# One order for all five queues, weight words joined in pairs, one reciprocal per head pair, and a warm-up

## The chip, the cores and the metric

The kernel runs on one core of one Trainium2 chip. The metric is the device time of one execution in microseconds (us); lower is better. The engines are named as in the profile: PE (TensorE matmul), PEld (its weight loads), DVE (VectorE), ACT (ScalarE), POOL (GpSimd) and SP (SyncE, which issues nearly all DMA transfers here).

## The reference, cut to what matters

Three stages follow each other: windowed attention, a dense gated block, and a top-1 mixture of eight experts.

```python
scores = q @ k.T / 8, masked to 0 <= i-j < 64       # 4 batches, 8 heads, 576 tokens, 64 dims
x = softmax(scores) @ v                             # as [2304, 512]
x = ((x @ w1) * (x @ w2)) @ w3 @ w_out              # weights arrive as 64-bit floats
e = argmax(x @ w_gate); gate = softmax(x @ w_gate)[e] * sigmoid(x @ w_output_gate)[e]
out = gate * (relu(x @ ew1[e]) @ ew2[e])
```

## The kernel before, in words

**The dense block.** `w3 @ w_out` is multiplied once into one matrix, `w34`. Tokens go in six units (u = 0 to 5) of 384. For each unit and each of eight column blocks m, `gate` (L565) makes `x @ w1` and then `x @ w2` in two PSUM banks (tag `ab`), ACT keeps the first (`a_sb`, L570), DVE multiplies (L573), ACT and DVE write the product as a high and a low part (L577, L581), and `down` (L589) multiplies it by `w34`. Every float32 product is three passes over high and low parts.

**The weights.** `w_out`, `w3`, `w1` and `w2` come in 40 transfers of 512 KB (`fetch`, L494), of 64-bit words. For each, DVE joins float32 values out of the two halves of a word in three operations over 512 elements (`convert`, L511, L513, L518), through a PSUM bank of tag `ab`; ACT writes the high part (L532) and POOL the low part (L536). The product `w34` is made of the 24 transfers of `w_out` and `w3` (L545). `w1` takes over the SBUF of the raw `w3` words and `w2` that of the finished `w_out`, so `w2` is written only when the product is complete; then the units start.

**Attention.** There are 16 head pairs, four for each batch. One pair has three groups g: scores (L149 adds the mask in the matmul, L153), a row maximum on DVE (L162, L165), exponentials on ACT (L175), sum plus 1e-9 and its reciprocal on DVE (L185, L187, once per group), the product on POOL (L192), a transpose on PE and its copy on ACT (L199, L204), and with v the output (L216) in PSUM, of which ACT and DVE write high and low parts into the units' `x` tiles (L228, L232). `x` has three buffers, so unit u shares one with unit u+3. Pairs 4 to 7 (batch 1) write into units 1 and 2. Two buffers each hold q, k and v: the load of v for pair n waits until the output of pair n-2 is done.

**Routing.** Every token's row is scattered into the DRAM buffer `xs`, from which the experts read. Before that, 32 transfers of 257 KB (`clear`, L813) fill the head of every expert's part with blank rows.

**Order.** A planner (`Plan`) keeps a list of steps with an engine, a length, a rank, and buffers that it takes and gives back, and emits them in the order in which it would start them. Before, PE alone kept that order (`manual_schedule(engines={E.PE})`); the instructions of DVE, ACT, POOL and SP were placed anew by the framework's own scheduler. An engine runs its instructions strictly in the order in which they stand, and SP's transfers are issued in order too: one that waits holds those behind it.

Of the kernel before, what the change touches and what calls it, by code (L numbers as in the profile page):

```python
# [29 lines left out]
NTILE = NT // 128  # L30
NEG = -1.0e30
RING = 3
NB = S // 64
VW = NB * 128

# [83 lines left out]
class Attention:  # L119
# [11 lines left out]
    def __init__(self, tc, pool, ps_s, ps_v, qkv, xunit, ident):  # L131
        self.tc, self.nc, self.pool, self.ps_s, self.ps_v = tc, tc.nc, pool, ps_s, ps_v
        self.qkv, self.xunit, self.ident = qkv, xunit, ident
        self.s = {}
        self.idb, self.mask = masks(tc.nc, pool, ident)
# [31 lines left out]
    def exps(self, n, g):  # L167
        nc, s = self.nc, self.s[n]
        ps = s["S", g]
        nm = s.pop(("nm", g))  # L170
        p = s["p", g] = self.pool.tile([128, self.GW], F32, name="pp", tag="pp", bufs=3)
        rs = s["rs", g] = self.pool.tile([128, 3], F32, name="rs", tag="rs", bufs=4) if n < self.SUMS else None
        for i in range(3):
            o = slice(128 * i, 128 * i + 128)
            nc.scalar.activation(out=p[:, o], in_=ps[:, o], func=AF.Exp, bias=nm[:, i:i + 1], scale=0.125,  # L175
                                 **({} if rs is None else dict(accum_out=rs[:, i:i + 1])))

    def recip(self, n, g):
        nc, s = self.nc, self.s[n]
        ps = s.pop(("S", g))  # L180
        rs = s.pop(("rs", g))
        if rs is None:
            rs = ps[:, 392:395]
            nc.vector.tensor_reduce(out=rs, in_=s["p", g].rearrange("p (a b) -> p a b", a=3), axis=AX, op=ALU.add)
        nc.vector.tensor_scalar(ps[:, 400:403], rs, 1e-9, None, op0=ALU.add)  # L185
        r = s["r", g] = self.pool.tile([128, 3], F32, name="r", tag="r", bufs=4)
        nc.vector.reciprocal(out=r, in_=ps[:, 400:403])  # L187
# [46 lines left out]
    def plan(self, P, n, r, done):  # L234
# [8 lines left out]
        for i, x in enumerate("qkv"):  # L243
            add(x, "DMA", (1.5, 0.8, 1.5)[i], -18 + i, self.load, (), i, take=[(x, (x, n))], lat=2.0)
        for g in range(3):
            q = -12 + 2 * g
            late = n >= self.LATE
            add(("sc", g), "PE", 0.38 if late else 0.55, q, self.score, N("q", "k"), g, take=[("S", ("S", n, g))],
                give=[("q", n), ("k", n)] if g == 2 else [])
            add(("top", g), "DVE", 1.28 if late else 0.72, q, self.top, N(("sc", g)), g)  # L250
            add(("exp", g), "ACT", 1.65 if n < self.SUMS else 1.02, q, self.exps, N(("top", g)), g, take=[("pp", ("pp", n, g))])
            add(("rec", g), "DVE", 0.4 if n < self.SUMS else 0.9, q, self.recip, N(("exp", g)), g, give=[("S", n, g)])
            add(("nor", g), "POOL", 0.85, q, self.normal, N(("rec", g)), g)
# [17 lines left out]
def masks(nc, pool, ident):  # L271

    idb = pool.tile([128, 128], BF16, name="idb")
    nc.vector.tensor_copy(idb, ident)
    mask = [pool.tile([128, 3, 128], BF16, name=f"mask{x}") for x in range(2)]
    nc.gpsimd.memset(mask[1], 0.0)
    for h in range(2):

        a = mask[1][64 * h:64 * h + 64]
        nc.gpsimd.affine_select(out=a, in_=a, pattern=[[0, 3], [1, 128]], compare_op=ALU.is_ge,  # L280
                                fill=NEG, base=-1, channel_multiplier=-1)
        nc.gpsimd.affine_select(out=a, in_=a, pattern=[[0, 3], [-1, 128]], compare_op=ALU.is_ge,
                                fill=NEG, base=64, channel_multiplier=1)
    nc.gpsimd.tensor_copy(mask[0], mask[1])
    nc.gpsimd.memset(mask[0][:, 0, 0:64], NEG)
    return idb, mask
# [127 lines left out]
def attention_moe_moe_kernel(ctx: ExitStack, tc: tile.TileContext, q0, k0, v, w1, w2, w3, w_out,  # L414
# [13 lines left out]
    ps_ab = pool(ctx, "ps_ab", bufs=2, space=PSUM)  # L428
    ps_acc = pool(ctx, "ps_acc", bufs=UT, space=PSUM)
    ps_s = pool(ctx, "ps_s", bufs=2, space=PSUM)  # L430
    ps_v = pool(ctx, "ps_v", space=PSUM)

# [14 lines left out]
    make_identity(nc, ident)  # L447
    gates = const.tile([128, 4, 16], F32, name="gates")
    rt = Router(tc, const, xs)

    moe = pool(s_moe, "moe")
    pa = pool(s_pa, "pa")
    att = pool(s_att, "att", side="right")
# [10 lines left out]
    at = Attention(tc, att, ps_s, ps_v, (q0, k0, v), xunit, ident)  # L464
    for src, c in ((w_gate, 0), (w_ogate, 8)):
        nc.sync.dma_start(out=gates[:, :, c:c + 8], in_=src.rearrange("(k p) e -> p k e", p=128))
    P = Plan(dict(q=2, k=2, v=2, S=2, pv=1, ab=2, acc=UT, pp=3, PT0=1, PT1=1, PT2=1, ck=RING, f=3, ck2=3,
                  w3T=3, a_sb=2, gt=2, x2=3, x2T=1))
# [6 lines left out]
    STAGED = {"wo": 8, "w3": 8}  # L475

    seq = [("wo", 0), ("w3", 0), ("wo", 1), ("wo", 2), ("wo", 3), ("w3", 2), ("wo", 4), ("w3", 1), ("wo", 5),
           ("wo", 6), ("wo", 7)]
    seq += [("w3", j) for j in range(3, 16)] + [("w1", j) for j in range(4)]
    seq += [(x, j) for j in range(8) for x in ("w2", "w1") if x == "w2" or j > 3]  # L480
# [4 lines left out]
    def fetch(i):  # L485
        kind, c = seq[i]
        if c < STAGED.get(kind, 0):
            t = stage[kind][c // 4][:, 1024 * (c % 4):1024 * (c % 4) + (1024 if wide else 512)]
            t = t.bitcast(I32 if wide else F32)
        else:  # L490
            t = ckp.tile([128, 1024 if wide else 512], I32 if wide else F32, name="ck", tag="ck", bufs=RING)
        raw[i] = t
        src = half[kind][c]
        nc.sync.dma_start(out=t, in_=src.bitcast(I32) if wide else src)  # L494
# [7 lines left out]
    def convert(i, step):  # L502

        if not wide:
            if step == 2:
                f32s[i] = raw.pop(i)
            return
        word = raw[i].rearrange("p (c t) -> p c t", t=2)
        if step == 0:
            bits[i] = ps_ab.tile([128, 512], F32, name="bits", tag="ab").bitcast(I32)  # L510
            V.tensor_scalar(bits[i], word[:, :, 1], 3, 0x3FFFFFFF, op0=ALU.logical_shift_left, op1=ALU.bitwise_and)  # L511
        elif step == 1:
            V.scalar_tensor_tensor(out=bits[i], in0=word[:, :, 1], scalar=-0x40000000, in1=bits[i],  # L513
                                   op0=ALU.bitwise_and, op1=ALU.bitwise_or)
        else:
            del raw[i]
            f32s[i] = ckp.tile([128, 512], F32, name="f", tag="f", bufs=3)
            V.scalar_tensor_tensor(out=f32s[i].bitcast(I32), in0=word[:, :, 0], scalar=29, in1=bits.pop(i),  # L518
                                   op0=ALU.logical_shift_right, op1=ALU.bitwise_or)
# [3 lines left out]
    def parts(i):  # L523
        kind, c = seq[i]
# [6 lines left out]
    def high(i):  # L531
        nc.scalar.activation(out=parts(i)[0], in_=f32s[i], func=AF.Copy)  # L532

    def low(i):
        hi, lo = parts(i)
        nc.gpsimd.tensor_tensor(lo, f32s.pop(i), hi.bitcast(F32), op=ALU.subtract)  # L536
# [22 lines left out]
    def gate(u, m, k):  # L559
        x, w = xunit(u), ws[("w1", "w2")[k]]  # L560
        ps = gps[u, m, k] = ps_ab.tile([128, 512], F32, name="ab", tag="ab")[:, 0:UNIT]
# [202 lines left out]
    def plan_chunk(i, kind, c):  # L764
        r = 5 + 2.4 * i
        staged = c < STAGED.get(kind, 0)
        key = ("ck", i)
        L = P.add("DMA", 1.4, r - 10, lambda: fetch(i), take=() if staged else [("ck", key)], lat=2.0)
        old = [done["mm", x, 3] for x in range(16)] if kind == "w2" else []
        t0 = P.add("DVE", 0.6, r, lambda: convert(i, 0), [L] + old, take=[("ab", ("b", i))])  # L770
        t1 = P.add("DVE", 0.6, r, lambda: convert(i, 1), [t0], lat=0)
        t2 = done["read", kind, c] = P.add("DVE", 0.6, r, lambda: convert(i, 2), [t1], take=[("f", ("f", i))],
                                           give=[("b", i)] + ([] if staged else [key]))
        after = [t2] + ([done["read", "w3", x] for x in range(8)] if kind == "w1" else [])
        hi = P.add("ACT", 0.63, r + 2, lambda: high(i), after, take=[("w3T", ("w3T", c))] if kind == "w3" else [])
        done[kind, c] = P.add("POOL", 1.28, r + 3, lambda: low(i), [hi], give=[("f", i)])

    def plan_w34(c, r):
        m, g = divmod(c, 2)
        for j in range(4):  # L780
            done["mm", c, j] = P.add(
                "PE", 0.71, r, lambda j=j: w34_mm(c, j), [done["w3", c], done["wo", 4 * g + j]]
                + ([done["mm", c - 1, 3]] if g else []),
                take=[("acc", ("accw", m))] if g == 0 and j == 0 else [], give=[("w3T", c)] if j == 3 else [])
# [5 lines left out]
    for n in range(NP):  # L790
        at.plan(P, n, 24 + 11 * n, done)
    for i, x in enumerate(seq):
        if x[0] != "w2":
            plan_chunk(i, *x)
    for c in range(16):
        plan_w34(c, 11 + 2.4 * seq.index(("w3", c)))
# [4 lines left out]
    def start_mo():  # L801
# [3 lines left out]
        z = blank[0] = mo[0].tile([128, RW], F32, name="x2", tag="x2", bufs=3)  # L805
        nc.gpsimd.memset(z[:, 0:DM], 0.0)
        nc.gpsimd.memset(z[:, DM:RW], float(NT))

    blank = [None]

    def clear(e, j):
        r = NS * e + 128 * j
        nc.sync.dma_start(out=xs[r:r + 128, :], in_=blank[0])  # L813

    def side(u):
# [3 lines left out]

    mo_open = P.add("SP", 0.0, 0, start_mo, [done["mm", x, 3] for x in range(16)], lat=0)  # L820
    done["clear"] = [P.add("DMA", 1.45, 106 + 3 * i, lambda i=i: clear(*divmod(i, 4)), [mo_open],
                           take=[] if i else [("x2", "blank")], give=["blank"] if i == 4 * NE - 1 else [])
                     for i in range(4 * NE)]
# [55 lines left out]
    def plan_end():  # L879

        o = P.add("SP", 0.0, 0, open_exp, [done["x", n] for n in range(B * NP)], lat=0)
        for j in range(11):
            done["el", j] = P.add("DMA", 1.4, 400 + 5 * j, lambda j=j: eload(j + 1), [o], take=[("ck2", ("ck2", j))], lat=2.0)
        for j in range(8):

            k, c = divmod(j, 4)
            old = [done["gate", NU - 1, 2 * c + 1, k - 1]] if k else []
            h = P.add("ACT", 1.06, 400 + 5 + 5 * j, ehigh, [done["el", j]] + old + ([done["es", j - 1]] if j else []))
            done["es", j] = P.add("DVE", 1.22, 400 + 5 + 5 * j, elow, [h], give=[("ck2", j)])
# [253 lines left out]
```

## Time and profile before

| | |
|---|---|
| median of 3 runs | 767.65 us (766.26 to 767.84) |
| the profiled execution | 768.43 us, its span 766.6 us |
| mean granted TensorE clock | 0.987 of full |
| busy: PE, DVE, ACT, POOL | 721.9 (94%), 370.9, 296.8, 165.0 us |
| unit 0's first gate starts, its last down is followed at | 98.79 us, 171.45 us |
| moved by DMA | 105.76 MB |

Busy time counts an engine's instructions; a PE that is busy may still run at half its clock, and matmuls overlap each other. What is lost on PE shows as idle time before an instruction with the name of what ended it, and as a matmul that takes longer than its fellows. A transfer has an issue on SP's queue and a landing, which is later by the time that the transfers in front of it take.

### The profile page before, as it was taken

To read this page: it belongs to the slowest core of one execution; us is meant where nothing else is said; L and a number is where in the kernel's file an instruction comes from. 1 tells how busy PE (TensorE), PEld (TensorE's weight loads), DVE (VectorE), ACT (ScalarE), POOL (GpSimd) and SP (SyncE) were. 2 spreads that over 40 slices of the span, in tenths; PEclk is the share of its full clock that TensorE was granted. 3 is DMA by queue.
4 is the path that set the end of the run, shared out by engine and by line. 5 is a ranking of instruction groups with operands and counts; after the bars stand their busy time and mean duration, and the time that the engine had idled before them with its cause. 6 is when DMAs were issued, how large, how long until landed. Compare 5 with 4: busy or idle time off the path is not lost. (4 is left out here: it accounts for less than half of the span.)

```text
span 766.6 us, 12408 instructions
## 1 busy us (share of the span) xinstructions
PE 721.9 (94%) x4630; PEld 644.8 (84%) x4630; DVE 370.9 (48%) x862; ACT 296.8 (39%) x697; POOL 165.0 (22%) x230
## 2 busy tenths in 40 slices
PE   3689899999999999999999999999999999999996
PEld 2568688989999989999999998878888897988875
DVE  6797668533255645574532233645255461671101
ACT  2466354541134334333411213446354463563121
POOL 5455444300111211131010010432112011111010
PEclk9899899999999999999999999999999999999999
DMA  8858588960112322210500011476546772740000
GB/s 333 344 193 285 200 241 276 272 187 3 42 48 81 107 94 81 80 73 1 192 30 14 1 70 40 160 246 225 187 144 209 239 247 76 255 157 28 4 29 27
DMA packets 39393, 105.76 MB, mean 138 GB/s; under 512 B 5388, under 2 KB 5388, under 8 KB 39312
## 3 DMA queue, kind: packets, MB, share of 16 engines
q1 hardware_dynamic: 36112, 95.27, 37.9%
q0 software_dynamic: 3200, 9.46, 3.1%
q8 instruction: 45, 0.74, 0.4%
q14 instruction: 36, 0.29, 0.1%
HBM read 86.83 MB, written 18.93 MB: 138 GB/s over the span
## 5 line engine op out<-in xcount | busy, mean ns | idle before, releaser
L565 PE MATMUL ab<-xt,w 128*128 128x384 f32 x1152 | 219.5, 341 | 2.7 <-DVE f L518 2.3
L565 PEld LDWEIGHTS ab<-xt,w 128*128 128x128 f32 x1152 | 199.4, 189 | 5.2 <-DVE f L518 2.5
L589 PE MATMUL acc<-w,gt 128*128 128x512 f32 x432 | 112.2, 403 | 0.7 <-ACT gt L577 0.7
L589 PEld LDWEIGHTS acc<-w,gt 128*128 128x128 f32 x432 | 79.5, 190 | 17.5 <-DVE gt L581 1.0
L933 PE MATMUL yps<-w,hT 128*128 128x512 f32 x336 | 82.6, 396 | 0.0
L192 POOL TENSOR_TENSOR pp<-pp,r 128x384 f32<-128x384 f32 x48 | 40.0, 834 | 157.3 <-DVE r L187 64.2
L933 PEld LDWEIGHTS yps<-w,hT 128*128 128x128 f32 x336 | 61.3, 188 | 11.8
L573 DVE TENSOR_TENSOR a_sb<-ab,a_sb 128x384 f32<-128x384 f32 x48 | 26.7, 557 | 90.8 <-PE ab L565 84.5
L175 ACT ACTIVATE pp<-sps,nm 128x128 f32<-128x128 f32 x144 | 46.8, 368 | 50.4 <-DVE nm L165 50.4
L545 PE MATMUL wps<-w,w3T 128*128 128x512 f32 x192 | 53.2, 423 | 12.3 <-ACT w3T L532 12.1
L690 DVE TENSOR_TENSOR w<-ck,w 128x1024 fp32r<-128x1024 f32 x45 | 54.4, 1221 | 20.4 <-ACT w L686 19.7
L686 ACT ACTIVATE w<-ck 128x1024 fp32r<-128x1024 f32 x48 | 50.1, 1057 | 18.5 <-DMA ck<-in_moe_w 16.6
L577 ACT ACTIVATE gt<-a_sb 128x384 fp32r<-128x384 f32 x48 | 25.1, 523 | 82.9 <-DVE a_sb L573 82.8
L925 POOL DMA_INDIRECT out<-y,idx x20 | 19.6, 979 | 173.8 <-ACT y L924 119.7
L545 PEld LDWEIGHTS wps<-w,w3T 128*128 128x128 f32 x192 | 36.8, 201 | 20.4 <-ACT w3T L532 12.1
L957 PEld LDWEIGHTS hps<-exT,w 128*128 128x128 f32 x384 | 46.3, 192 | 4.9 <-issue 3.1
L957 PE MATMUL hps<-exT,w 128*128 128x256 f32 x384 | 47.3, 284 | 3.2 <-PEq L1086 1.4
L570 ACT ACTIVATE a_sb<-ab 128x384 f32<-128x384 f32 x48 | 23.6, 492 | 57.2 <-PE ab L565 56.3
L204 ACT ACTIVATE PT<-tps 128x384 f32<-128x384 f32 x48 | 23.5, 493 | 46.4 <-PE tps L199 46.4
L438 DVE TENSOR_TENSOR exT<-gps,exT 128x512 fp32r<-128x512 f32 x23 | 15.8, 691 | 52.4 <-ACT exT L437 52.4
L153 PE MATMUL sps<-k,q 128*128 128x128 f32 x288 | 41.1, 282 | 0.0
L153 PEld LDWEIGHTS sps<-k,q 128*128 128x128 f32 x288 | 39.1, 198 | 0.6
(137 smaller groups left out, 1014.2 us busy)
## 6 DMA issues: line engine op xcount, KB each, us to landing
ck<-in_moe_w SPq DMA_DIRECT2D x88, 512.0 KB, 4.5
q<-in_q SPq DMA_DIRECT2D x16, 576.0 KB, 5.6
v<-in_v SPq DMA_DIRECT2D x16, 576.0 KB, 3.9
xs<-x SPq DMA_DIRECT2D x32, 257.0 KB, 8.7
xg<-xs SPq DMA_DIRECT2D x29, 257.0 KB, 3.0
k<-in_k SPq DMA_DIRECT2D x16, 320.0 KB, 6.2
w<-in_moe_w_out SPq DMA_DIRECT2D x8, 512.0 KB, 8.5
w<-in_moe_w SPq DMA_DIRECT2D x8, 512.0 KB, 9.8
```

The lines of the kernel that those rows point to most:

```text
L153: nc.tensor.matmul(ps[:, 128 * i:128 * i + 128], lhsT=s["q"][:, 128 * c:128 * c + 128], rhs=s["k"][:, 64 * c:64 * c + 128], start=late, st ...
L175: nc.scalar.activation(out=p[:, o], in_=ps[:, o], func=AF.Exp, bias=nm[:, i:i + 1], scale=0.125, **({} if rs is None else dict(accum_out=r ...
L192: nc.gpsimd.tensor_tensor(p, p, s.pop(("r", g)).unsqueeze(2).to_broadcast([128, 3, 128]), op=ALU.mult)
L545: mm(ps, lhsT=t[:, a, 128 * j:128 * j + 128], rhs=wo[b][:, o:o + 512], start=g == 0 and j == 0 and x == 0, stop=g == 1 and j == 3 and x == 2)
L565: mm(ps, lhsT=w[a][:, c:c + 128], rhs=x[:, b, kk, :], start=kk == 0 and i == 0, stop=kk == 3 and i == 2)
L573: V.tensor_tensor(asb[u, m], gps.pop((u, m, 1)), asb[u, m], op=ALU.mult)
L577: nc.scalar.activation(out=g[:, 0, :], in_=asb[u, m], func=AF.Copy)
L589: mm(accs[u][t], lhsT=g[:, a, 128 * t:128 * t + 128], rhs=ws["w34"][b][:, 512 * m:512 * m + 512], start=m == 0 and i == 0, stop=m == 7 and ...
L686: nc.scalar.activation(out=eparts()[0], in_=eq[0], func=AF.Copy)
L690: low.tensor_tensor(lo, eq.popleft(), hi.bitcast(F32), op=ALU.subtract)
L933: mm(ps, lhsT=hT[f][:, a, c0:c0 + 128], rhs=w[b][:, 512 * f:512 * f + 512], start=f == 0 and i == 0, stop=f == 7 and i == 2)
L957: mm(ps[:, 0:256], lhsT=w1e[a][:, c:c + 128], rhs=xT[:, b, kk, 0:256], start=kk == 0 and i == 0, stop=kk == 3 and i == 2)
```

## The change

- All queues follow the planner up to the last unit (`manual_schedule` for DVE, ACT, POOL and SP as well). Its ranks are new: the first pairs from rank 12 at steps of 6.1, pairs 4 to 7 from 68, unit 0 from 61, unit 1 from 134, and what follows 40 earlier.
- `w3` and `w_out` words are joined two transfers at a time: the first two operations run over 1024 elements in two PSUM banks of their own (`bits`), given up for `ab` when all of `w3` and `w_out` is read; the third stays at 512.
- Pairs 0 to 7 have one sum plus 1e-9 and one reciprocal over nine columns in place of three over three.
- The blank rows come from the `x` tile of unit 2, filled at the start, not from a tile that exists once the product is complete. `done["free", 2]` makes the first writes into that `x` tile wait for all 32 clears.
- Twelve matmuls on zeros run at the start; the small gate weights are loaded on ACT's queue; the masks are built without DVE; four buffers for the exponentials in place of three; the second half of expert 0's weights waits for the last column block of unit 5.

```diff
+WARM = 12
...
+CLEAR = 94
+MERGE = True
+CH = 2.47
+A0, DA0, A1, DA1 = 12, 6.1, 68, 9.6
+U0, DU0, U1 = 61, 10, 134
...
+        if one:
+            add("rec", "DVE", 0.36, -8, self.recip, N(*[("exp", g) for g in range(3)]), 2, give=[("S", n, 2)])
...
+        for _ in range(WARM):
+            mm(cold, lhsT=warm[:, 0:128], rhs=warm, start=True, stop=True)
...
+        t = P.add("DVE", us, r, lambda: convert(i, 0), L, take=[(tag, ("b", i))], lat=0)
+        t = P.add("DVE", us, r, lambda: convert(i, 1), [t], lat=0)
+        for c in cs:
...
+            t = done["read", kind, c] = P.add("DVE", 0.69, r, lambda c=c: join(i, c), [t],
+                                              take=[("f", ("f", i, c))], give=give, lat=0)
...
-        z = blank[0] = mo[0].tile([128, RW], F32, name="x2", tag="x2", bufs=3)
...
+    blank = xunit(2).rearrange("p a b c -> p (a b c)")[:, 0:RW].bitcast(F32)
...
+    done["clear"] = [P.add("DMA", 0.75, CLEAR + i, lambda i=i: clear(*divmod(i, 4))) for i in range(4 * NE)]
+    done["free", 2] = P.add("SP", 0.0, 0, lambda: None, done["clear"], lat=0)
...
-    done["clear"] = [P.add("DMA", 1.45, 106 + 3 * i, lambda i=i: clear(*divmod(i, 4)), [mo_open],
...
-    plan_unit(0, 100, 8)
-    plan_unit(1, 166, 6.5)
+    plan_unit(0, U0, DU0)
+    plan_unit(1, U1, 6.5)
...
-    P.run()
+    with tc.manual_schedule(engines={E.DVE, E.Activation, E.Pool, E.SP}):
+        P.run()
```

On SP's queue, from pair 5's q load on (`xs` is a clear, `ck` and `w0` weight transfers, `q`, `k`, `v` loads of attention), the changed kernel has:

```order
L881 DMA xs_57<-xt2_152 128x514
L152 DMA q_726<-in_q0 128x1152
L152 DMA k_742<-in_k0 128x640
L881 DMA xs_57<-xt2_152 128x514 x11
L152 DMA v_856<-in_v 128x1152
L881 DMA xs_57<-xt2_152 128x514 x7
L539 DMA ck_932<-in_moe_w1 128x1024
L881 DMA xs_57<-xt2_152 128x514 x2
L539 DMA ck_969<-in_moe_w2 128x1024
```

Nineteen of the clears stand ahead of `w1`'s fourth transfer here, and the last of the 32 stands behind `w2`'s fourth. Before, the first clear stands behind `w2`'s fourth transfer:

```order
L494 DMA ck_979<-in_moe_w2 128x1024
L494 DMA ck_1010<-in_moe_w2 128x1024
L494 DMA ck_1021<-in_moe_w2 128x1024
L494 DMA ck_1134<-in_moe_w2 128x1024
L813 DMA xs_57<-x2_1067 128x514 x6
L141 DMA q_1264<-in_q0 128x1152
L494 DMA ck_1173<-in_moe_w2 128x1024
```

So the clears moved ahead of the `w2` transfers that they followed. On ACT, about the first gates of unit 0 (`a_sb` is the kept first product, `w2` the high part of `w2`, `xt2` and `xt1` the `x` of units 2 and 1, `gt` the high part of the product), the changed kernel has:

```order
L624 ACTIVATE a_sb_1186<-ab_1133 128x384
L586 ACTIVATE w2_1149<-f_1160 128x512
L245 ACTIVATE xt2_152<-pvt_1163 128x64
L245 ACTIVATE xt1_378<-pv_1162 128x192
L245 ACTIVATE xt2_152<-pv_1162 128x320
L586 ACTIVATE w2_1149<-f_1205 128x512
L631 ACTIVATE gt_1236<-a_sb_1120 128x384
```

Pair 4's pieces of `x`, whose first goes into the tile of the blank rows, stand ahead of the first `gt` of unit 0, and that first piece waits for the landing of the last clears on all the DMA semaphores. Before, two `gt` stand ahead of them, and they wait for PE alone:

```order
L577 ACTIVATE gt_1216<-a_sb_1106 128x384
L532 ACTIVATE w2_1124<-f_1184 128x512
L204 ACTIVATE PT_1235<-tps3_1223 128x384
L532 ACTIVATE w2_1124<-f_1221 128x512
L577 ACTIVATE gt_1255<-a_sb_1150 128x384
L175 ACTIVATE pp_1259,rs_1260<-sps_1229,nm_1253 128x128 x3
L228 ACTIVATE xt1_359<-pv_1268 128x192
L228 ACTIVATE xt2_1312<-pvt_1269 128x64
L228 ACTIVATE xt2_1312<-pv_1268 128x320
```

The pieces moved up past unit 0's first `gt`, and gained a wait.

## Rows read from the trace of the kernel before

**Rows 1.** Waits of PE up to 172 us: total us, times, longest
```profile
PE wps L545 <- ACT w3T L532: 12.1, 1, 12.1
PE tps L199 <- POOL pp L192: 8.4, 4, 3.7
PE ab L565 <- DVE f L518: 2.3, 1, 2.3
```

**Rows 2.** Timeline of PE: start us, us, instructions, idle before
```profile
12.09 2.15 PE L545 MATMUL wps<-w,w3T 128*128 128x512 f32 x3 [12.09 <-ACT w3T L532]
...
92.51 0.90 PE L199 MATMUL tps<-ident,pp 128*128 128x128 f32 x3 [3.69 <-POOL pp L192]
93.06 5.13 PE L545 MATMUL wps<-w,w3T 128*128 128x512 f32 x12
...
98.79 2.36 PE L565 MATMUL ab<-xt,w 128*128 128x384 f32 x12
...
104.10 0.83 PE L153 MATMUL sps<-k,q 128*128 128x128 f32 x6
...
111.00 2.35 PE L589 MATMUL acc<-w,gt 128*128 128x512 f32 x9
113.28 1.15 PE L216 MATMUL pv<-PT,v 128*64 128x64 f32 x32
...
171.45 2.25 PE L565 MATMUL ab<-xt,w 128*128 128x384 f32 x12
```

**Rows 3.** Stretches: length, busy us (instructions) by engine, clock, DMA share, GB/s
```profile
15.00:30.00 15.00, 8.44 (x43) 6.07 (x41) 13.27 (x30) 8.00 (x28) 9.94 (x9) 0.87 1.03 421
...
90.00:105.00 15.00, 12.49 (x62) 10.94 (x63) 6.09 (x17) 4.68 (x18) 4.98 (x7) 0.77 0.59 180
```

**Rows 4.** Timeline of DVE: the first weight transfer, and a reciprocal
```profile
5.93 0.69 DVE L511 TENSOR_SCALAR bits<-w 128x512 int32<-128x512 int32 x1 [4.97 <-DMA w<-in_moe_w_out]
...
20.25 0.17 DVE L187 RECIPROCAL r<-sps 128x3 f32<-128x3 f32 x1
```

**Rows 5.** Groups of instructions: busy us, mean ns of one, idle before
```profile
L690 DVE TENSOR_TENSOR w<-ck,w 128x1024 fp32r<-128x1024 f32 x45 | 54.4, 1221 | 20.4 <-ACT w L686 19.7 <-PE hps L957 0.7
L573 DVE TENSOR_TENSOR a_sb<-ab,a_sb 128x384 f32<-128x384 f32 x48 | 26.7, 557 | 90.8 <-PE ab L565 84.5 <-PE tps L199 3.5 <-PE rps L375 2.7
L581 DVE TENSOR_TENSOR gt<-a_sb,gt 128x384 fp32r<-128x384 f32 x48 | 29.5, 615 | 11.8 <-ACT gt L577 11.7
L162 DVE TENSOR_REDUCE sps<-sps 128x3 f32<-128x384 f32 x48 | 26.7, 560 | 7.1 <-PE sps L153 6.8
```

**Rows 6.** DMA issues of the whole run: count, KB each, median us to landing
```profile
ck<-in_moe_w SPq DMA_DIRECT2D x88, 512.0 KB, 4.5
q<-in_q SPq DMA_DIRECT2D x16, 576.0 KB, 5.6
v<-in_v SPq DMA_DIRECT2D x16, 576.0 KB, 3.9
xs<-x SPq DMA_DIRECT2D x32, 257.0 KB, 8.7
...
k<-in_k SPq DMA_DIRECT2D x16, 320.0 KB, 6.2
```

**Rows 7.** A stretch in which seven clears, one v and one q are issued, columns as above
```profile
140.00:150.00 10.00, 10.00 (x91) 9.18 (x90) 3.68 (x12) 3.68 (x13) 2.44 (x3) 1.00 1.06 250
```

**Rows 8.** Timeline of SP's queue: start us, us of the issue
```profile
1.86 0.50 SPq L494 DMA_DIRECT2D w<-in_moe_w_out  x1
...
23.04 0.33 SPq L141 DMA_DIRECT2D k<-in_k  x1
33.69 0.33 SPq L141 DMA_DIRECT2D v<-in_v  x1
```

**Rows 9.** Timeline of ACT: first and last of a pair's three pieces into x
```profile
142.47 0.33 ACT L228 ACTIVATE xt<-pv 128x192 fp32r<-128x192 f32 x1
...
142.80 0.45 ACT L228 ACTIVATE xt<-pv 128x320 fp32r<-128x320 f32 x1
```

More of the change, by code (lines that the diff above doesn't have):

```diff
@@ L529, in parts, with high, low @@
         return [t[:, 512 * c:512 * c + 512] for t in dest(kind)]
[L531 to L536, printed above, removed]
+    def high(kind, c):
+        nc.scalar.activation(out=parts(kind, c)[0], in_=f32s[kind, c], func=AF.Copy)
+    def low(kind, c):
+        hi, lo = parts(kind, c)
+        nc.gpsimd.tensor_tensor(lo, f32s.pop((kind, c)), hi.bitcast(F32), op=ALU.subtract)
     def w34_mm(c, j):
@@ L760, in early_low, with plan_chunk @@
         V.tensor_tensor(xTs[0][:, 1, 0:4, o], tps.pop(("e", j)), xTs[0][:, 0, 0:4, o].bitcast(F32), op=ALU.subtract)
[L764 to L776, printed above, removed]
+    def plan_chunk(i, kind, cs):
+        r = CH * sum(len(x[1]) for x in seq[:i])
+        n = len(cs)
+        us = 0.69 if n == 1 else 1.22
+        key = ("w3p" if kind == "w3" and n == 2 else "ck", i)
+        L = [P.add("DMA", 1.25 * n, r - DQ, lambda: [fetch(i, c) for c in cs],
+                   take=[] if kind == "wo" or (kind == "w3" and n == 1) else [(key[0], key)], lat=2.0)]
+        if kind == "w2":
+            L += [done["mm", x, 3] for x in range(16)]
+        tag = "bits" if kind in stage else "ab"
+        if tag == "ab":
+            L.append(done["start_ab"])
+        t = P.add("DVE", us, r, lambda: convert(i, 0), L, take=[(tag, ("b", i))], lat=0)
+        t = P.add("DVE", us, r, lambda: convert(i, 1), [t], lat=0)
+        for c in cs:
+            give = ([("b", i)] + ([key] if kind not in stage or (kind == "w3" and n == 2) else [])) if c == cs[-1] else []
+            t = done["read", kind, c] = P.add("DVE", 0.69, r, lambda c=c: join(i, c), [t],
+                                              take=[("f", ("f", i, c))], give=give, lat=0)
+            after = [t] + ([done["read", "w3", x] for x in range(16)] if kind == "w1" else [])
+            hi = P.add("ACT", 0.63, r + 2, lambda c=c: high(kind, c), after,
+                       take=[("w3T", ("w3T", c))] if kind == "w3" else [])
+            done[kind, c] = P.add("POOL", 1.28, r + 3, lambda c=c: low(kind, c), [hi], give=[("f", i, c)])
@@ L882, in plan_end @@
         for j in range(11):
[L883 removed]
+            done["el", j] = P.add("DMA", 1.4, 360 + 5 * j, lambda j=j: eload(j + 1), [o], take=[("ck2", ("ck2", j))], lat=2.0)
         for j in range(8):
             k, c = divmod(j, 4)
[L887 to L888 removed]
```

204 lines of the change are left out of this document (124 added, 80 removed).

## The prediction, made before the changed kernel was run

> **What bounds the kernel now.** I read the busy shares first: PE is busy for 94% of the span, and all five queues are changed only up to the last unit, so the question is where PE loses time before that, and whether the change gives it back. The waits of PE up to 172 us [rows 1] answer that: 12.1 us until the first product of weights starts, 8.4 us in four waits for POOL's products before the transposes, and 2.3 us for a joined word of w2. Up to unit 0's last down (what follows it starts at 171.45 us [rows 2]) nearly all of that is over, which is why I take this point for the comparison. PE also runs slowly after a long idle time: the twelve matmuls behind the 3.69 us wait take 5.13 us, 0.43 us each, while 12 of 384 columns take 2.36 us in the next part, about 0.26 us for 512 columns; that is 2 us [rows 2]. The granted clock of that stretch is 0.77 in the mean of both levels, 1.2 and 2.4 GHz [rows 3].
>
> Then the stretches by engine: from 15 to 30 us DVE is busy for 13.27 of 15 us and the DMA share is 1.03, at 421 GB/s [rows 3]. So the beginning is fed by a full DMA queue and a nearly full DVE. Last I read SP's queue: it stands for 10.65 us between a k load at 23.04 us and the v load at 33.69 us [rows 8], because that v needs the buffer of a finished pair, and all transfers behind it stand too.
>
> **The parts of the change.** The first weight transfer is issued at 1.86 us behind the two gate loads [rows 8], which now go out on ACT's queue, and DVE starts on it at 5.93 us [rows 4], 4.1 us later. Issued at about 0.8 us, it is ready at 4.9, and without the small DVE operations between the first two words PE can start near 10 us and not at 12.09 [rows 2]: 2 us. The warm-up is on an idle PE; whether the clock is still up at 10 us the trace can't show, so it is worth 0 to 1.3 us (three matmuls took 2.15 us there [rows 2], against 0.8 at full clock). I take 0.
>
> Joining two words: an operation over 1024 elements takes 1.22 us [rows 5], two over 512 take 1.38 [rows 4]. That is 0.16 us in each of two operations in ten pairs: 3.2 us less on DVE. The bound below is a loss: the operations of one pair now follow each other and each needs the last one's result. One reciprocal per pair leaves out 32 small operations of 0.17 us [rows 4], 5.4 us. In return the first group's product waits for the third group's exponentials; the matmuls of w34 have to cover that, and if they don't it costs a wait as the four of 8.4 us [rows 1].
>
> The order is the large part. Pair by pair, PE now has the same matmuls (and the 12 of the warm-up), so what it can win is its waits. Past the start these are 15.6 us in all groups of that view, the largest of which are in rows 1, and some 2 us for each of four slow stretches as the one above: about 24 us.
>
> **What takes the place of the waits.** The 32 clears are moved ahead, and pair 4's first piece of x on ACT now waits for all of them to land. Behind it on ACT stand w2's third high part and unit 0's first gt; behind the matching low piece on DVE stands the first product of unit 0. So PE can make four gates and three groups of scores, and then its first down waits for the last clear. When does that land? Ahead of it, and counting w2's fourth transfer before it, SP's queue has 32 weight transfers of 512 KB, seven q of 576, seven k of 320 and six v of 576 [rows 6]: 26,112 KB, 26.7 MB. At the 421 GB/s of a full queue [rows 3] that is 63.5 us.
>
> A clear has 257 KB [rows 6]. The trace has none alone. The nearest row is the stretch in which mostly clears run, 250 GB/s at a DMA share above 1 [rows 7]: 1.05 us each, 33.7 us for 32. From below, a clear at the read rate of 421 GB/s would take 0.63 us, 20 us in all; from above, if a v and a q (1.18 of that stretch's 2.5 MB) took 2.8 us at 421 GB/s, the other 1.32 MB, five clears, took 7.2 us: 1.44 us each, 46 us in all. I take 1.05, the row itself.
>
> So without a gap the last clear lands at 0.8 (first issue) + 63.5 + 33.7 + 2.8 (the 4.1 us from issue to use, less 1.3 of moving [rows 4, 8]) = 100.8 us. There are gaps: pair 2's v waits for pair 0's output as now. Twenty-one transfers stand ahead of it (13 weights, three q, three k, two v: 10.75 MB, 25.5 us), so the queue runs dry near 27 us, and by rows 8 that output comes near 33.7, less 2 us for the earlier start: 4 us of gap, and 1 for those that follow. The last clear lands at about 106 us.
>
> From there to PE: three pieces on ACT, 1.0 us [rows 9]; the last low piece and the product on DVE, 0.5 and 0.56; two maxima that stand in between, 1.2; the low part of gt, 0.62 [rows 5]; with the hand-overs 4.5 us. PE's first down starts near 110.5 us. What is left then is nearly what was left before at 113.28 us, where four gates were made too [rows 2]: one down more (2.3), one output (1.4) and two groups of scores (0.8 each) less [rows 2]. Before, it took 58.2 us to 171.45; so now 57.4, with the same small waits and one slow start after the idle time. Unit 0 ends at 167.9 us and not at 171.45: 3.5 us are won. After that PE waits for little before and after the change, so the profiled execution goes from 768.43 to 764.9 us, and the median, which is 0.8 us under that execution, to 764.
>
> Everything that DVE, the start and the earlier order win in front of that wait is hidden by it; it would count only if the clears landed before about 95 us.
>
> The Trainium skill, "DMA: Bandwidth & Descriptors", section "Anatomy of one DMA", has a transfer cost 2.0 us plus its bytes at 436 GB/s. By that a clear takes 0.60 us of moving, the last would land near 86 us, and the wait would vanish. The reads of this trace come near it (421 GB/s), the stretch of clears does not (250 GB/s), so I leave it to the rival below.
>
> **Rivals.** *The clears are in time.* For it speaks that the lower bound, 0.63 us, puts the last clear at 92 us with the gaps; against it, the 250 GB/s. Then PE reaches that down as fast as its own waits allow: before, the same amount was left at 171.45 - 57.4 = 114 us; less 2 for the start and about half of the 24 us of waits and slow stretches that is 100. Unit 0 ends at 157.4, 14 us earlier: 754, in the median 753.
>
> *SP's fixed order costs more than it gives (slower).* Each v stands in front of weights and clears, and before it held the queue for over 10 us once [rows 8]. If the gaps add up to 15 us and not to 5, the last clear lands at 116, the down starts at 120.5, and unit 0 ends at 178: 6.5 us later, 775, in the median 774. It is slower from a last landing at 109.6 us on, so 4 us of further gaps decide it. For it speaks that all of the outputs depend on chains over five queues that now can't step aside; against it, that 13 weight transfers stand in front of the first such wait.
>
> *No order is better than the other past unit 0.* In units 1 to 5 DVE and ACT now follow the planner strictly; a piece of x in front of a gt could hold PE's two banks as it does for pair 4. PE lost little there before; if every one of the eight pairs behind cost 1 us, the 3.5 are gone and 4.5 more: 772.
>
> **How the numbers follow.** Main case 0.52, its own range 759 to 771: clears from 0.95 to 1.2 us and gaps from 3 to 7 us move the last landing from 100.5 to 112.5. Clears in time 0.26. SP's gaps 0.16. Later stages 0.06. About 0.2%, 1.5 us, is what a measurement of this kernel tells from no change. Faster: 0.26 and 0.37 of the main case, 0.63. Same: 0.11 of the main case. Slower: 0.04 of it, 0.16 and 0.06, 0.26. The range is 750 to 775: it takes in the rivals and leaves out the ends of the clear's bounds.
>
> **What would show it.** Right: ACT's first piece of pair 4 (behind unit 0's second kept product) waits for DMA, its end near 106 us; PE idle for 8 to 14 us before its first down, which starts near 110; a slow stretch behind it; next unit 0's end near 168. The DMA share near 1 from 33 us to that landing, with a gap near 30. Wrong: the last clear landing before 95 us, or PE's first down released by the product itself; PE's first matmul of w34 later than 11 us; waits of PE in units 1 to 5.

## The result, and the profile of the changed kernel

The changed kernel takes 757.77 us (757.27 to 758.23, four runs) beside 767.33 us of the kernel before on the same chip: a ratio of 0.9877, 95% interval 0.986 to 0.9894. The forecast was 764.0 us. The range of 750 to 775 held; the main case's own range, 759 to 771, and the size did not: 3.5 us were forecast from one profiled execution to the other, 768.43 to 757.99 are 10.4.

PE's waits up to 172 us, in the columns of [rows 1]:

```profile
PE tps L216 <- POOL pp L209: 3.3, 4, 2.6
PE sps L160 <- DVE xt L249: 3.3, 1, 3.3
PE wps L599 <- ACT w3T L586: 3.1, 1, 3.1
```

The first product of weights starts at 9.62 us and not at 12.09; its wait is shorter still because the warm-up fills part of the time. The waits for POOL's products fell from 8.4 us to 3.3, and a wait is new, 3.3 us for DVE's piece of x. PE's timeline shows where they lie (the lines answer to [rows 2]):

```profile
9.62 1.18 PE L599 MATMUL wps<-w,w3T 128*128 128x512 f32 x2 [3.13 <-ACT w3T L586]
...
87.33 0.55 PE L216 MATMUL tps<-ident,pp 128*128 128x128 f32 x3 [2.56 <-POOL pp L209]
...
91.62 2.33 PE L619 MATMUL ab<-xt,w 128*128 128x384 f32 x12
...
104.85 0.32 PE L160 MATMUL sps<-mask,idb 128*128 128x384 bf16 x1 [3.29 <-DVE xt L249]
...
107.08 4.18 PE L619 MATMUL ab<-xt,w 128*128 128x384 f32 x12 [0.80 <-DVE a_sb L627]
111.06 2.72 PE L643 MATMUL acc<-w,gt 128*128 128x512 f32 x9
...
162.28 2.27 PE L619 MATMUL ab<-xt,w 128*128 128x384 f32 x12
164.39 2.24 PE L643 MATMUL acc<-w,gt 128*128 128x512 f32 x9
166.47 2.27 PE L619 MATMUL ab<-xt,w 128*128 128x384 f32 x12
```

The first down starts at 111.06 us, in the kernel before at 111.00 [rows 2]: the same, with two groups of scores and one output more already done. The gate behind the wait, the fourth, takes 4.18 us instead of 2.3. Unit 0's last down ends at 166.47, and by then one gate of unit 1 (at 162.28) is done too, which is work that lay behind 171.45 before.

What holds PE there is on ACT (the first line, a piece of pair 4's x, answers to [rows 9]) and on DVE:

```profile
104.31 0.22 ACT L245 ACTIVATE xt<-pvt 128x64 fp32r<-128x64 f32 x1 [6.04 <-DMA v<-in_v]
```

```profile
83.82 0.69 DVE L560 TENSOR_SCALAR bits<-ck 128x512 int32<-128x512 int32 x1 [3.89 <-DMA ck<-in_moe_w]
...
85.95 0.16 DVE L200 TENSOR_SCALAR sps<-rs 128x9 f32<-128x9 f32 x1
86.15 0.22 DVE L202 RECIPROCAL r<-sps 128x9 f32<-128x9 f32 x1
```

ACT stands for 6.04 us before the first piece. The page names a v load as its releaser, but what has to be done for that tile are the clears: the experiment own_blank below, in which the tile is another, has no such wait, and in a second execution of the changed kernel (after_again) the trace puts the same wait, 6.2 us, down to the clears themselves. DVE stands for the fourth word of w1 (the weight transfer behind nineteen clears in SP's order above; DVE's first word of w2 comes only after the product of the weights, at 91.66 us). The merged reciprocal for POOL's products stands behind that word in its queue, which gives PE's 2.56 us at 87.33. SP's queue shows what both wait for (lines as in [rows 8]):

```profile
57.34 10.27 SPq L881 DMA_DIRECT2D xs<-xt  x11
...
69.32 5.62 SPq L881 DMA_DIRECT2D xs<-xt  x7
75.56 0.34 SPq L539 DMA_DIRECT2D ck<-in_moe_w  x1
```

The word that DVE waits for is issued at 75.56 us, behind the eighteen clears of these lines, and used at 83.82. The view of the transfers between 60 and 98 us (its last line here: count, KB each, median us to landing, as in [rows 6]):

```profile
DMA packets 5272, 11.65 MB, mean 307 GB/s; under 512 B 583, under 2 KB 583, under 8 KB 5268
...
xs<-xt SPq DMA_DIRECT2D x27, 257.0 KB, 8.8
```

And the stretches of [rows 3], with the one behind them:

```profile
15.00:30.00 15.00, 12.89 (x99) 9.82 (x98) 13.88 (x23) 11.14 (x42) 9.14 (x9) 0.95 1.03 408
90.00:105.00 15.00, 11.71 (x97) 10.55 (x96) 7.69 (x15) 5.26 (x17) 4.20 (x5) 0.95 1.05 327
105.00:120.00 15.00, 14.20 (x68) 12.91 (x68) 11.47 (x24) 7.37 (x23) 7.38 (x7) 0.77 0.55 181
```

DMA is full up to about 105 us, and PE runs slowly behind the wait, at a mean granted clock of 0.77 of the upper of the two levels, 1.2 and 2.4 GHz.

### The profile page after: what moved, and what is told of

It is laid out like the page before. It is cut to its first block, busy times and chain, and to the rows that moved or that the text cites. A ratio compares the mean times of both kernels' runs of the same rounds, so it can differ in the third digit from the quotient of the medians.

```text
span 755.7 us, 12329 instructions
## 1 busy us (share of the span) xinstructions
PE 726.1 (96%) x4642; PEld 646.4 (86%) x4642; DVE 375.3 (50%) x810; ACT 297.7 (39%) x697; POOL 163.7 (22%) x231
## 5 line engine op out<-in xcount | busy, mean ns | idle before, releaser
L643 PE MATMUL acc<-w,gt 128*128 128x512 f32 x432 | 110.5, 400 | 0.0
L466 DVE TENSOR_TENSOR h<-tps,h 128x256 fp32r<-128x256 f32 x24 | 10.2, 424 | 56.1 <-ACT h L465 56.1
```

What stands on the lines that cost most here:

```text
L466: low.tensor_tensor(lo, src, hi.bitcast(F32), op=ALU.subtract)
L643: mm(accs[u][t], lhsT=g[:, a, 128 * t:128 * t + 128], rhs=ws["w34"][b][:, 512 * m:512 * m + 512], start=m == 0 and i == 0, stop=m == 7 and ...
```

## The experiments

Sixteen runs followed in four groups, each group on one chip beside the kernel before, whose median was 766.8 to 767.8 us; one of them is the changed kernel once more (after_again). The table has the changed kernel and all of them but before_gate7, which stands at its place below: the median, its ratio to the kernel before with the 95% interval, and from the profiled execution the start of PE's first down and the execution's own time.

| kernel | us | ratio | first down | that execution |
|---|---|---|---|---|
| changed kernel | 757.8 | 0.9877 (0.986 to 0.9894) | 111.06 | 757.99 |
| after_again (the same) | 760.6 | 0.9906 (0.9887 to 0.9925) | 113.63 | 761.03 |
| own_blank | 755.8 | 0.9853 (0.9833 to 0.9874) | 109.53 | 757.66 |
| clear8 | 767.5 | 1.0006 (0.999 to 1.0022) | 120.86 | 767.59 |
| dve_undone | 761.9 | 0.9943 (0.9927 to 0.996) | 115.00 | 761.62 |
| no_warm | 759.7 | 0.9913 (0.9896 to 0.993) | 110.82 | 758.82 |
| free_order | 762.8 | 0.9936 (0.9911 to 0.9962) | 116.50 | 762.80 |
| old_ranks | 760.6 | 0.9897 (0.9864 to 0.9931) | 115.48 | 762.51 |
| words_single | 760.7 | 0.9901 (0.987 to 0.9933) | 113.96 | 760.96 |
| clears_behind | 746.3 | 0.9716 (0.9684 to 0.9749) | 100.21 | 746.41 |
| behind_dve_undone | 750.7 | 0.9778 (0.9761 to 0.9795) | 103.74 | 750.48 |
| behind_free_order | 761.5 | 0.9927 (0.9899 to 0.9955) | 111.61 | 760.60 |
| behind_gates_first | 746.7 | 0.973 (0.9712 to 0.9748) | 100.45 | 746.67 |
| behind_sp_fixed | 754.7 | 0.9826 (0.9799 to 0.9853) | 108.24 | 755.42 |
| behind_words_single | 747.8 | 0.9736 (0.9709 to 0.9763) | 102.61 | 749.37 |
| behind_no_warm | 747.6 | 0.974 (0.9713 to 0.9767) | 100.18 | 748.10 |

In all rows the last column less the one before it is 646 to 649 us: the time is the start of the first down and, to within 3 us, a constant. In the kernel before it is 768.43 - 111.00 = 657.4. Two things limit what the rows can tell: the changed kernel itself differs by 2.8 us between its two sets of runs, and a profiled execution can lie up to 1.9 us off its own median (own_blank, old_ranks).

### own_blank and clear8: is it the clears' landing?

```diff
-    blank = xunit(2).rearrange("p a b c -> p (a b c)")[:, 0:RW].bitcast(F32)
+    blank = att.tile([128, RW], F32, name="blank")
```

> The changed kernel, with the blank rows of the 32 clears in a tile of their own and no longer in the tile of unit 2's x; the order on every queue stays the same. Theory (the last clear's landing holds PE's first down): ACT's 6.04 us of idle time before pair 4's first piece goes, PE's 3.29 us wait at 104.85 us goes, and so does the slow clock behind it (the fourth gate takes 2.1 us and not 4.18, the first down 2.3 and not 2.72): 3.3 + 2.1 + 0.4 = 5.8 us, 752.0 us against 757.8 of the changed kernel (750.5 to 754). Rival (the product or w2's last conversions come late anyway, and the landing was only the last of several things): at most 1 us, 756.8 to 757.8.

Neither came. The wait of 3.3 us is gone, but the time went to other places:

```profile
88.69 0.90 PE L216 MATMUL tps<-ident,pp 128*128 128x128 f32 x3 [4.20 <-POOL pp L209]
...
106.74 3.00 PE L619 MATMUL ab<-xt,w 128*128 128x384 f32 x12 [1.88 <-DVE a_sb L627]
```

The wait for POOL's product is 4.2 us here and not 2.56, since DVE stood 5.55 us, not 3.89, for w1's word, and the first down is only 1.5 us earlier. Part of that difference is chance: in after_again, where the tile is the old one, DVE stands 6.35 us for the same word, and against that execution the first down is 4.1 us earlier. So what the tile costs is 1.9 to 4.7 us in the medians and not known closer. DVE also stands 2.57 us for a later word, at 105.04 us, in front of the product that PE's 1.88 us wait for. What is clear is that the first down still starts at 109.53 us with no wait for the landing on ACT: the theory that the landing alone holds the down fell. In clear8, one clear in four went out a second time:

```diff
         nc.sync.dma_start(out=xs[r:r + 128, :], in_=blank)
+        if j == 0:
+            nc.sync.dma_start(out=xd[128 * e:128 * e + 128, :], in_=blank)
```

> The changed kernel with 8 more clears of the same size among the 32 (one of the first of each expert's four goes out a second time, into a tensor that nobody reads); order otherwise unchanged. Theory (landing holds the down): the last clear lands later by 8 x 0.94 us (117 ns a packet, 8 packets on each of 16 engines, from the changed kernel's trace) = 7.5 us, the first down starts at 118.5 us and not at 111.06, and the time is 757.8 + 7.5 = 765.3 us (763.5 to 767). If a clear costs 0.60 us, as the prediction worked out from the page's rule: +4.8, 762.6. Rival (landing does not bind): 757.8, within 1 us.

It was 767.5 us, beyond the theory's range. The eight clears cost 9.8 us against the first time of the changed kernel and 7.0 against the second, 0.9 to 1.2 us each. The added time stands in the very place that own_blank pointed to (PE, then DVE):

```profile
95.44 0.90 PE L216 MATMUL tps<-ident,pp 128*128 128x128 f32 x3 [10.71 <-POOL pp L209]
...
115.34 0.48 PE L160 MATMUL sps<-mask,idb 128*128 128x384 bf16 x1 [5.39 <-DVE xt L249]
```

```profile
91.93 0.69 DVE L561 TENSOR_SCALAR bits<-ck 128x512 int32<-128x512 int32 x1 [12.04 <-DMA ck<-in_moe_w]
...
94.26 0.22 DVE L202 RECIPROCAL r<-sps 128x9 f32<-128x9 f32 x1
```

A clear at the 0.60 us that the expectation names would have added 4.8 us; 7.0 is the least that was measured.

### clears_behind: the clears behind the weights

```diff
-    done["clear"] = [P.add("DMA", 0.75, CLEAR + i, lambda i=i: clear(*divmod(i, 4))) ...]
-    done["free", 2] = P.add("SP", 0.0, 0, lambda: None, done["clear"], lat=0)
+    late = [done["read", "w2", x] for x in range(8)]
+    done["clear"] = [P.add("DMA", 0.75, CLEAR + i, lambda i=i: clear(*divmod(i, 4)), late) ...]
```

with the tile of own_blank. The order of PE, DVE, ACT and POOL is that of the changed kernel. (The word that the expectation calls one of w2 is w1's fourth, as above; w2's words come behind it.)

> The changed kernel with the blank rows in a tile of their own and all 32 clears in one row behind w2's last transfer on SP's queue; the order on PE, DVE, ACT and POOL is unchanged. Theory now (the clears cost by standing in front of weight transfers: DVE's queue waits for a w2 word and holds the reciprocal behind it, so PE waits for POOL's product; taking away ACT's wait alone only moved the time there): in the changed kernel PE's 2.6 us wait at 84.8 us, its 3.3 us wait at 104.85, 0.8 at 107 and the slow stretches behind them (1.4 + 2.1 + 0.8 us) go, 9 to 11 us: 748 us (746 to 751). Rival (conversion work on DVE, ACT and POOL and not the transfers holds PE here): like own_blank, 754 to 757.

It was 746.3 us: the theory, to 2 us, and the fastest version here, 21 us under the kernel before and 9.5 under own_blank, from which only the place of the clears differs. The clears now stand in one row at the end of the weights on SP:

```profile
73.76 2.99 SPq L539 DMA_DIRECT2D ck<-in_moe_w  x2
...
118.91 0.33 SPq L539 DMA_DIRECT2D ck<-in_moe_w  x1
119.29 10.15 SPq L881 DMA_DIRECT2D xs<-blank  x13
```

PE's waits up to 172 us, the two largest, and a stretch. From 60 to 440 us PE has no wait at all, and DMA has time to spare; the word that the changed kernel used at 83.82 us is issued at 73.76 and used at 80.07, without a wait of DVE, and the reciprocal behind it runs at 82.39 us and not at 86.15:

```profile
PE wps L599 <- ACT w3T L586: 4.4, 1, 4.4
PE tps L216 <- POOL pp L209: 1.3, 4, 0.6
```

```profile
60.00:75.00 15.00, 15.00 (x106) 12.23 (x105) 14.15 (x24) 7.59 (x21) 8.13 (x8) 1.00 0.18 62
```

### DVE's savings: dve_undone, words_single, behind_dve_undone, behind_words_single

```diff
-            V.tensor_scalar(bits[i], word[:, :, 1], 3, 0x3FFFFFFF, ...)
+            for o in range(0, n, 512):
+                V.tensor_scalar(bits[i][:, o:o + 512], word[:, o:o + 512, 1], 3, 0x3FFFFFFF, ...)
...
-        nc.vector.tensor_scalar(ps[:, 400:400 + b - a], rs, 1e-9, None, op0=ALU.add)
-        nc.vector.reciprocal(out=r[:, 0:b - a], in_=ps[:, 400:400 + b - a])
+        for o in range(0, b - a, 3):
+            nc.vector.tensor_scalar(ps[:, 400 + o:403 + o], rs[:, o:o + 3], 1e-9, None, op0=ALU.add)
+            nc.vector.reciprocal(out=r[:, o:o + 3], in_=ps[:, 400 + o:403 + o])
```

and the second operation of a joined pair as the first; words_single has only the upper part.

> The changed kernel with DVE's two savings undone in place: the two operations of a joined pair of words are four over 512 elements again, and the one reciprocal of a head pair is three again; the order of everything else is unchanged. That is 20 x 0.16 + 32 x 0.17 = 8.6 us more on DVE. Theory (what DVE saves is hidden by the landing): first down still at 111 us, 757.8 us within 1 us. Rival (DVE sets the pace of the first 90 us and its savings are the gain): 3 to 8 us more, 761 to 766.

> The changed kernel with only the joined operations undone in place (four over 512 elements for two over 1024 in each of ten pairs, 3.2 us more on DVE); the reciprocals stay merged. With both undone the time was 4 to 5 us more than the changed kernel's. Theory (DVE sets the pace while words are converted, up to 60 us): nearly all of it here, 760.5 to 762 us. Rival (the reciprocals matter, since three of them stand in front of POOL's products): 757.8 to 759 us.

> clears_behind (746.3 us, PE without a wait from 50 us on) with DVE's two savings undone as in dve_undone, 8.6 us more on DVE. Theory (DVE sets the pace up to 60 us, where it is busy for 13 to 14 of 15 us): 2 to 4 us more, 748.5 to 750.5. Rival (DVE's time told only through the late transfers): 746.3 to 747.3 us.

> clears_behind with only the joined operations undone (3.2 us more on DVE); with the reciprocals undone too it was 4.3 us slower. Theory (DVE sets the pace while words are converted): 2.5 to 3.5 us more, 748.8 to 749.8 us. Rival (the reciprocals hold POOL's products): 746.3 to 747.3 us.

With the clears in front, dve_undone is 4.1 us over the first time of the changed kernel and 1.3 over the second, and words_single equals the second: not decided, since the same kernel differs by 2.8 us between two sets of runs. With the clears behind, both savings are worth 4.3 us (750.7 against 746.3, from two sets of runs), a little above the theory. The joined words alone come to 1.5 us, between the two expectations, which would leave 2.8 for the reciprocals; but the intervals of that run and of clears_behind overlap, and the first downs of the profiled executions part it the other way (102.61 - 100.21 = 2.4 us for the words, 1.1 for the reciprocals). How the 4.3 us divide is not shown. The trace of dve_undone says how DVE's time reaches the landing itself. Waits of SP's queue from 5 to 60 us, first in the changed kernel, then in dve_undone:

```profile
SPq L152 <- PE pvt L233: 11.1, 3, 5.4
SPq L539 <- DVE f L573: 5.7, 4, 2.4
```

```profile
SPq L152 <- PE pvt L234: 12.6, 3, 5.6
SPq L540 <- DVE f L577: 9.1, 4, 4.0
```

SP stands for buffers that DVE empties. A slower DVE makes later transfers late, the clears too: the first of them is issued at 57.70 us and not at 54.41 (54.02 in after_again), and the first down starts at 115.00.

### The order: free_order, behind_free_order, behind_sp_fixed

```diff
-    with tc.manual_schedule(engines={E.DVE, E.Activation, E.Pool, E.SP}):
-        P.run()
+    P.run()
```

behind_sp_fixed keeps E.SP in that list.

> The changed kernel without the fixed order on DVE, ACT, POOL and SP up to the last unit: the scheduler orders them again, while PE's order stays; on SP the two orders are the same, on DVE, ACT and POOL they differ (924, 403 and 62 rows). Theory (the fixed order is a part of the gain): PE's waits for POOL's products come back, 8 us of them were before; 762 to 766 us. Rival (the gain is in DVE's savings and the start): 757.8 us within 1.5 us.

> clears_behind without the fixed order on DVE, ACT, POOL and SP. Theory (the fixed order is worth 5 us as in free_order, most of it in front of 30 us): 750 to 753 us. Rival (it was worth that only together with transfers that came late): 746 to 748 us.

> clears_behind with the fixed order on SP (and PE) alone; DVE, ACT and POOL are ordered by the scheduler, as in behind_free_order. There the scheduler also put 8 clears back in front of w2's first word on SP. Theory (the 15 us of behind_free_order are those clears): 748 to 751 us. Rival (they are the order of DVE, ACT and POOL): 757 to 761 us.

free_order is 2.2 to 5.0 us slower than the changed kernel, as the theory had it. behind_free_order came out beyond both expectations, 15.2 us over clears_behind: the scheduler also put clears back in front of weight words, eight of them in front of the word issued at 79.09 us, for which DVE then stands 3.02 us. behind_sp_fixed lies between its two expectations and parts the two causes: 8.4 us for the order on DVE, ACT and POOL, 6.8 more for SP's own order with those clears. The stretches from 15 to 45 us, first of clears_behind, then of behind_sp_fixed, show what the order does:

```profile
15.00:30.00 15.00, 13.30 (x99) 10.36 (x99) 13.79 (x23) 11.16 (x42) 9.07 (x9) 0.91 1.02 403
30.00:45.00 15.00, 13.32 (x102) 9.87 (x101) 12.75 (x26) 9.19 (x31) 9.17 (x9) 1.00 0.98 372
```

```profile
15.00:30.00 15.00, 11.59 (x81) 9.07 (x81) 10.62 (x22) 8.16 (x31) 7.45 (x7) 0.84 0.98 398
30.00:45.00 15.00, 12.52 (x67) 9.34 (x63) 10.31 (x19) 8.62 (x30) 7.79 (x8) 0.88 0.82 294
```

DVE does 3.2 and 2.4 us less in them, buffers come free later, and the queue moves 294 GB/s where it moved 372.

### The start and the warm-up: no_warm, behind_no_warm, behind_gates_first

```diff
-WARM = 12
+WARM = 0
```

```diff
-        nc.scalar.dma_start(out=gates[:, :, c:c + 8], ...)
+        nc.sync.dma_start(out=gates[:, :, c:c + 8], ...)
```

> The changed kernel without the twelve warm-up matmuls; order otherwise unchanged. Theory (everything in front of the landing is hidden): first product of weights still near 9.6 us, three matmuls of it at most 1.3 us slower, first down still at 111 us, 757.8 us within 0.8 us. Rival (the warm-up brings the clock up earlier and this is part of the gain): 1.5 to 3 us more, 759.3 to 760.8.

> clears_behind without the twelve warm-up matmuls. In no_warm the difference (759.7 us) lay inside the spread of the changed kernel itself (757.8 and 760.6 us). Theory (no price, since the first products of weights wait for words and not for PE): 746.3 us within 0.7. Rival (a slow clock on the first products moves all that follows): 747.8 to 749 us.

> clears_behind with the two gate loads in front of the first weight transfer on SP's queue again, as before. Theory (the beginning is fed by a full queue, so a later first transfer moves all): the first product of weights starts 1.1 to 2 us later, 747.3 to 748.3 us. Rival (hidden by other waits in front of 50 us): 746.3 us within 0.7.

no_warm lies between the two times of the changed kernel and decides nothing. behind_no_warm is 1.3 us over clears_behind, between the expectations, but not by the warm-up: its first down starts at 100.18, against 100.21. The first products of w34 take the same with the warm-up (first line, clears_behind) and without it:

```profile
9.76 2.15 PE L599 MATMUL wps<-w,w3T 128*128 128x512 f32 x3 [4.40 <-ACT w3T L586]
```

```profile
9.65 2.16 PE L599 MATMUL wps<-w,w3T 128*128 128x512 f32 x3 [9.65 <-ACT w3T L586]
```

With the gate loads first, PE's first product starts at 11.49 us, 1.7 later, and the first down at 100.45, 0.24 later: the start is hidden.

### After 200 us: old_ranks, before_gate7, after_again

old_ranks has the due times of units 2 to 5 and of the end at their old values (`179 + 53` to `219 + 53`, `174 + 14` to `214 + 14`, `360` to `400`).

> The changed kernel with the due times of units 2 to 5, of their pairs and of the end stage at their old values (40 us later); nothing before unit 1 changes. In the two traces the lead of the changed kernel grows from 7 us near 200 us to 10.6 at the end. Theory (the earlier due times give those 3.5 us): 760.5 to 761.5 us. Rival (they come from instruction supply and other things that the due times do not touch): 757.8 us within 1 us.

> The changed kernel itself, beside the three below. In old_ranks the trace loses 4.3 us more than the changed kernel's by its first down, where nothing was changed, and gains the same 4.7 to 4.9 us later. If that loss is how the transfers in front of the first down land on one chip or another, this run has 758.5 to 761 us and the old due times are worth less than 1 us; if the due times are worth 2.8 us, this run has 757.8 us within 0.7.

> The kernel before with one edit of the end stage alone: the high part of a word of the first expert's second half waits for the last unit's gate 7 and not for gate 2c+1. Theory (the 1.3 us that the changed kernel gains near 480 us are PE's waits of 0.66 and 0.41 us for ACT's gt and the early x, which stand behind those parts): both waits are gone and the time is about 1.1 us under the kernel before. Rival (they come from another edit): both waits still there, no difference.

old_ranks and after_again have the same median: the due times are worth nothing that can be told, and the expectation of 760.5 to 761.5 us was met for a wrong reason, the spread between sets of runs. before_gate7 is the kernel before with one edit:

```diff
-            old = [done["gate", NU - 1, 2 * c + 1, k - 1]] if k else []
+            old = [done["gate", NU - 1, 7, k - 1]] if k else []
```

It has 765.6 us, a ratio of 0.9973 (0.9957 to 0.9988). PE near 480 us, first in the kernel before, then in this one, then in the changed kernel:

```profile
475.18 2.26 PE L589 MATMUL acc<-w,gt 128*128 128x512 f32 x9
...
478.98 2.68 PE L589 MATMUL acc<-w,gt 128*128 128x512 f32 x9 [0.66 <-ACT gt L577]
...
482.19 1.22 PE L957 MATMUL hps<-xt,wx 128*128 128x256 f32 x8 [0.41 <-DVE xt L760]
483.25 0.60 PE L606 MATMUL xps<-ident,x 128*128 128x128 f32 x4
```

```profile
474.43 2.26 PE L589 MATMUL acc<-w,gt 128*128 128x512 f32 x9
...
477.32 2.35 PE L589 MATMUL acc<-w,gt 128*128 128x512 f32 x9
479.51 1.22 PE L957 MATMUL hps<-xt,wx 128*128 128x256 f32 x9
480.65 0.66 PE L606 MATMUL xps<-ident,x 128*128 128x128 f32 x4
```

```profile
467.01 2.24 PE L643 MATMUL acc<-w,gt 128*128 128x512 f32 x9
...
473.24 0.66 PE L660 MATMUL xps<-ident,x 128*128 128x128 f32 x4
```

Both waits are gone, by that edit alone: the theory, with 1.1 us of waits and 0.8 around them. From the down of the first line to the transposes of the last the kernel before takes 8.07 us, this one 6.22 and the changed kernel 6.23. The other 0.75 us of its lead are there at the first line already, where nothing was changed, and are chance.

## Why the prediction was wrong

**The start** was right in time, 9.62 us for "near 10", and the warm-up's zero was right. Behind_gates_first shows besides that with the clears behind the start does not matter.

**The wait at the first down** was right in its cause and its end, not in its length. ACT's first piece of pair 4 waits for the clears, its end is near 104.5 where 106 was forecast, and the down starts at 111.06 for 110.5. But PE stands for 3.29 and 0.80 us there and not for "8 to 14": it came late itself, by the wait for POOL's product at 87.33 and the slow matmuls behind it, which the prediction did not trace to the clears. And from the start of that piece to the down it took 6.8 us, where 4.5 were counted, since the fourth gate, which was to be done before the wait, stands behind it and takes 4.18 us. That the down starts within 0.6 us of the forecast is in part luck. The price of a clear, taken from [rows 7] as 1.05 us, holds: if, from 60 to 98 us, five words, a v, a q and a k (4.1 MB) go at 421 GB/s and take 9.8 us, 27 clears take the other 28.2, 1.04 each. The Trainium skill, "DMA: Bandwidth & Descriptors", "Anatomy of one DMA", gives 2.0 us plus the bytes at 436 GB/s, for the path from GpSimd; by it a clear would move in 0.60 us, an estimate. These clears, on SP's queue, disagree with it. (The 86 us that the prediction has by that rule leave out its own 5 us of gaps.)

**The step that failed first** is "What is left then is nearly what was left before", "with the same small waits and one slow start": 57.4 us were taken from the down to unit 0's end. Measured are 166.47 - 111.06 = 55.4, and these hold a gate of unit 1, 2.1 us, that the count left out: 53.3 (53.0 in after_again). The 58.2 us of before held a wait of 2.3 us and two slow groups behind it, together 3.9 us:

```profile
116.87 3.16 PE L565 MATMUL ab<-xt,w 128*128 128x384 f32 x12 [2.32 <-DVE f L518]
119.83 3.05 PE L589 MATMUL acc<-w,gt 128*128 128x512 f32 x9
```

In the changed kernel PE has no wait between the first down and unit 0's end, and only that down itself is a little slow, 2.72 us. The prediction named these waits and then kept them. That is 4.1 of the 6.9 us by which the gain was too small, less the 0.6 by which the down itself was later than forecast.

**The second** is "After that PE waits for little before and after the change". Of the 10.4 us, 171.45 - (166.47 - 2.1) = 7.1 are won up to unit 0's end, and 3.3 later. 1.8 of these lie near 480 us, where before_gate7 wins the same with one edit; the diff showed that edit and no term was given to it. Up to the down in front of it (475.18 and 467.01 us) 1.1 us are won, spread over units in which PE has no wait up to 440 us, and 0.4 come later still; these 1.5 us stay open. Waits on PE's own sequencer from 440 us on are 1.2 us shorter in the changed kernel (4.9 and 3.7), but they are between 2.3 and 5.3 in the others here and not shown to be the change.

The second set of runs, 760.6 beside 767.8 us, gains 7.3 us and not 9.6, and its first down starts 2.6 us later. Both terms are off there too: 53.0 us from the down to unit 0's end, and 2.6 us won behind it.

**What was wrong in the reasons** weighs more than either size. "Everything that DVE, the start and the earlier order win in front of that wait is hidden by it" took the landing as a sum of bytes over one rate and 5 us of gaps that DVE had no part in. It is not: SP's queue stands for buffers that DVE and PE empty, so a slower DVE moves the landing itself (dve_undone: ACT's first piece at 109.36 us and not 104.31 or 106.88). With the clears behind, where no landing holds PE, the order is worth 8.4 us and DVE's savings 4.3, and the earlier start, by behind_gates_first, nothing that can be told. And ACT's wait was not the only place: taking it away gave 1.9 to 4.7 us (own_blank), taking the clears out of the way as well 11.5 to 14.2 (clears_behind). The clears hold the weight words behind them, a word holds DVE's queue, and a reciprocal that stands behind it holds PE. The change is a sum of about 21 us won and 11 to 14 given back by where its clears stand and which tile they read.

**The rivals.** "The clears are in time": no, they were not; its 753 us, without the clears' wait, is 7 us above what clears_behind reached with them out of the way. "SP's fixed order costs more than it gives": the kernel is not slower, and the last clear landed at about 104 us, not 116. The rival looked at v loads in front of weights, while the clears stood there. "Later stages": PE has no wait from 172 to 440 us.

## What to carry to other kernels

When a transfer that nobody needs soon is moved ahead in a full queue, look at what stands behind it on the queue and then at what stands behind that on each in-order engine; the wait need not show on the reader of that transfer. Do not price a queue's landing as bytes over rate where the queue itself waits for buffers: what empties the buffers sets a part of it. And compare two orders at a point where the same work is done, not at the same event: here the same down started at 111.0 us in both.

## What the runs showed of the hardware

Writes of 2056-byte rows (514 float32 values) from SBUF to DRAM went at some 60% of the rate of the reads: 28 clears and one v between 122 and 152 us in clears_behind are 265 GB/s at a DMA share of 1.08; with the v taken at 421 GB/s, the rate of reads [rows 3], a clear takes 1.02 us, an estimate, which is 258 GB/s; whether the direction or the length of a row does it was not tried. The same program took 757.3 to 758.2 us in one set of runs and 759.1 to 762.3 in another, where its first down started 2.6 us later; DVE's wait for the word behind the clears carries such a difference into the time (3.89 and 6.35 us of waiting).
